# Batch 0's gated feed-forward in seven products instead of eight, and what moves on VectorE, GpSimd and the DMA queue for it

## The chip, the cores and the metric

One core of one Trainium2 chip runs the whole program. The metric is the device time in microseconds (us), median over several executions. Kernels of one call run on the same chip, with fresh runs of the kernel before among them.

## The reference, cut to what matters

```python
# q, k, v: (8 batches, 12 heads, 448, 64); w_gate, w_val: (768, 1536); w_out: (1536, 768)
scores = scale * q @ k.T - log(S);  attn = sigmoid(scores) @ v
x = attn as (8*448, 768)
y = (maximum(x @ w_gate, 0) * (x @ w_val)) @ w_out
```

The kernel takes four heads at a time: "block" n is four heads of one batch, three blocks to a batch, so batch 1 is blocks 3 to 5 and block 6 opens batch 2. The attention of batch b+1 ("visits") is spread among the feed-forward products of batch b.

The feed-forward has one trick. `x @ [w_gate, w_val]` and `h @ w_out` are done as 2 by 2 block products in the Strassen-Winograd way: seven block products instead of eight, with sums of the inputs, differences of the weights and sums of the results made on VectorE. "Product (g, k)" is product k of seven in group g of six.

## The kernel before: the parts that matter

Batch 0 uses plain products (eight), as the weights have only just arrived. Its stage is a time plan: each matmul has a cost, and loads, casts, visits and weight differences are dropped in between.

```python
def load_w(kind, j, half):                 # half a group of gate or value weights, staged as fp32
    st = swp.tile([P, WH], FP32, tag="sw") # five staging buffers of their own
    nc.sync.dma_start(st..., src...)
def cast_w(kind, j, half, eng): ...        # GpSimd casts it to fp16
def load_cast_out(f, eng):                 # one row of w_out: load, cast
    st = stp.tile([P, 2, S], FP32, tag="st")
    nc.sync.dma_start(flat, moe_w_out[f * P : (f + 1) * P, :])
    eng.tensor_copy(wo[:, f], flat)

def feed(i):                               # with each attention visit: what the next block needs
    ...
        if c == 4:
            dma_transposes(m)              # blocks 6 and later; blocks 4 and 5 go through TensorE
            if m == NPRO: order.extend(("o", f, 0) for f in range(NFC))   # then the rows of w_out
    if c == 4 and NPRO <= m + 1 < NB:
        load_all(m + 1)

for step, cost in enumerate(ffn0()):       # batch 0: plain products
    t += cost
    if order and (...): start_next()       # a load and its cast
    if due and t >= due[0]: visit()
    if wdue and t >= wdue[0]: gv_weights(*wsums.pop(0))
sums(("x", 1), [3, 2, 1, 4])               # input sums of batch 1, after all of batch 0
```

In a seven-product group the relu goes to one buffer, `r1`, and the first output product goes to GpSimd.

```python
elif k == 2: nc.scalar.activation(tmp(key, "r1")[:], ps, AF.Relu)          # bufs=1
elif k == 3: ...; nc.gpsimd.tensor_tensor(out=..., in0=r1, in1=s1, op=mult)
```

Of the kernel before, what the change touches and what calls it, by code (L numbers as in the profile page):

```python
# [16 lines left out]
def kernel(  # L17
# [10 lines left out]
    nc = tc.nc  # L28
# [21 lines left out]
    swp = ctx.enter_context(tc.tile_pool(name="swp", bufs=5))  # L50
# [14 lines left out]
    free = [0, 1]  # L65
# [20 lines left out]
    WH = NDC * FG * P // 2  # L86
# [3 lines left out]
    hT = wpool.tile([P, NFC, NHALF * S], FP16, name="hT")  # L90

# [6 lines left out]
    xT: dict = {}  # L98

# [44 lines left out]
    def load_w(kind: str, j: int, half: int):  # L144

        st = swp.tile([P, WH], FP32, tag="sw", name=f"st_w{kind}")
        w, r0 = moe_w_gate if kind == "g" else moe_w_val, half * NDC // 2 * P
        src = w[r0 : r0 + NDC // 2 * P, j * FG * P : (j + 1) * FG * P]
        nc.sync.dma_start(st[:].rearrange("p (c f) -> p c f", f=FG * P), src.rearrange("(c p) f -> p c f", p=P))
        staged[kind, j, half] = st  # L150

    def cast_w(kind: str, j: int, half: int, eng):
        st = staged.pop((kind, j, half))
        n = NDC // 2
        dst = (wg if kind == "g" else wv)[j][:, half * n : (half + 1) * n].rearrange("p c f -> p (c f)")
        eng.tensor_copy(dst, st[:])

    def load_cast_out(f: int, eng):

        st = stp.tile([P, 2, S], FP32, tag="st", name="st_wo")  # L160
        flat = st[:].rearrange("p r s -> p (r s)")[:, 0:DM]
        nc.sync.dma_start(flat, moe_w_out[f * P : (f + 1) * P, :])
        eng.tensor_copy(wo[:, f], flat)  # L163
# [11 lines left out]
    def transposes(n: int, nm: str, *engines, cut=(0, NCH)):  # L175
        h16 = qk16.pop((nm, n))
        if n <= NBLK:
            bank = take()
            tr = banks[bank][:, 0:S]
        else:  # L180
            bank = None
            tr = next_pair()[:, 0, 0:S]
        tr = tr.bitcast(FP16).rearrange("p (c h k) -> p c h k", c=NCH, h=2)
# [8 lines left out]
        if bank is not None:  # L192
            give(bank)
# [23 lines left out]
    def values(n: int, chunks):  # L217
        if chunks[0] == 0 and n not in PT:
            if n < NBLK:
                PT[n] = [banks[2][:, :], banks[3][:, :]]  # L220
# [17 lines left out]
        if chunks[-1] == NCH - 1:  # L238
# [12 lines left out]
            v16.pop(n)  # L251


    MM_US = 0.189

    begun: dict = {}

    def gv_part(b: int, f: int, w, dcs):

        key = (b, f, w is wg)  # L260
        if key not in begun:
            begun[key] = take()
        j, jj = divmod(f, FG)
        for dc in dcs:
            nc.tensor.matmul(  # L265
                banks[begun[key]][:, 0:S],
                w[j][:, dc, jj * P : (jj + 1) * P],
                xT[b, dc // 3][:, dc % 3],
                start=(dc == 0),
                stop=(dc == NDC - 1),  # L270
            )
        return begun[key]

    def up(b: int, f: int, gate_done=0, val_first=0):
        if val_first:
            gv_part(b, f, wv, range(val_first))
        for dc in range(gate_done, NDC):
            gate = gv_part(b, f, wg, [dc])
            if dc < NDC - 1:
                yield MM_US  # L280
        g_sb = tmpp.tile([P, S], FP32, tag="s2", name="gate_sb")
        if f < NFC // 2:
            nc.vector.tensor_scalar(out=g_sb[:], in0=banks[gate][:, 0:S], scalar1=0.0, scalar2=None, op0=AOP.max)
        else:
            nc.scalar.activation(g_sb[:], banks[gate][:, 0:S], AF.Relu)
        give(gate)
        yield MM_US
        for dc in range(val_first, NDC):
            val = gv_part(b, f, wv, [dc])
            if dc < NDC - 1:  # L290
                yield MM_US
        o = (b % NHALF) * S
        nc.vector.tensor_tensor(
            out=hT[:, f, o : o + S], in0=g_sb[:], in1=banks[val][:, 0:S], op=AOP.mult
        )
        give(val)
        yield MM_US
# [21 lines left out]
    def gv_weights(k: int, j: int):  # L319
# [8 lines left out]
        if i % 2 == 0:  # L328
            T["tile"] = swp.tile([P, 2, HDC, FG * P], FP16, tag="sw", name="Tw")
        T[k, j] = T["tile"][:, i % 2]  # L330
# [5 lines left out]
    def out_weights(k: int, part: int):  # L336
# [9 lines left out]
        elif k == 4:  # L346
            t = T["tile"][:, 1].rearrange("p c f -> p (c f)").rearrange("p (r m) -> p r m", m=HM)[:, 0:2]
# [119 lines left out]
    def out_product(pair: int, k: int):  # L467
# [29 lines left out]
        def store(t, m0, m1):  # L497
            for half in range(2):
                b, r = divmod((pair + t) * P + 64 * half, S)
                rows = out[b * S : (b + 1) * S].rearrange("(p c) m -> c p m", c=NCH)  # L500
                eng = nc.scalar if half and final and m0 == 0 and t == 1 else nc.sync
# [12 lines left out]
        elif k == 2:  # L514
            nc.scalar.activation(y(0)[:, 0:HM], ps, AF.Copy, scale=OUT_SCALE)
            give(i)
            if final:
                store(0, 0, HM)
        elif k == 3:
            scaled(y(0)[:, HM:DM], ps, live[key, "s1"][:, 0:HM])  # L520
            give(i)
            store(0, HM if final else 0, DM)
# [8 lines left out]
    def ffn(b: int, two_pairs):  # L531

        todo = [(0, 1), (0, 6), (0, 7), (0, 2), (0, 5), (1, 1), (0, 3)]
        for g in range(1, HFC):
            todo += [(g, 6), (g - 1, 4), (g, 7), (g, 5), (g, 2)]
            todo += [(g + 1, 1), (g, 3)]
        todo += [(HFC - 1, 4)]
        p, q_ = two_pairs
        for g, k in todo:
            if g == HFC:  # L540

                out_product(p, 1)
                yield OUT_US, False
                continue
            gv_product(b, g, k)
            if g == HFC - 1 and k == 5:
                sums(("h", p), [3])
            if g == HFC - 1 and k == 4:
                sums(("h", p), [2, 1, 4])
            yield GV_US, k in (2, 6)  # L550
        for i, k in (
            [(p, 7), (p, 2), (p, 6), (q_, 1), (p, 5), (q_, 6), (p, 3), (p, 4)]
            + [(q_, 7), (q_, 5), (q_, 2), (q_, 3), (q_, 4)]
        ):
            out_product(i, k)
            if (i, k) == (p, 6):
                sums(("h", q_), [3, 2])
            if (i, k) == (p, 5):
                sums(("h", q_), [1])
            if (i, k) == (p, 3):  # L560
                sums(("h", q_), [4])
            if b + 1 < B:
                if (i, k) == (q_, 5):
                    sums(("x", b + 1), [3, 2, 1])
                if (i, k) == (q_, 3):
                    sums(("x", b + 1), [4])
            yield OUT_US, True
# [3 lines left out]

    def cast_block(n: int):
        cast_qk(n, "q", nc.gpsimd)
        cast_qk(n, "k", nc.gpsimd)
        cast_v(n, nc.gpsimd)

    def feed(i: int):
# [3 lines left out]
        if NPRO <= m < NB:  # L581
# [6 lines left out]
            if c == 4:  # L588
                dma_transposes(m)
                if m == NPRO:  # L590
                    order.extend(("o", f, 0) for f in range(NFC))
        if c == 4 and NBLK < m < NPRO:
            later.append(m)
        if c == 4 and NPRO <= m + 1 < NB:
            load_all(m + 1)

    later: list = []
# [24 lines left out]

    zeros = hT[:, 0, 0:512]
    nc.vector.memset(zeros, 0.0)

    def filler(*widths):

        for w in widths:
            nc.tensor.matmul(banks[2][:, 0:w], zeros[:, 0:P], zeros[:, 0:w], start=True, stop=True)

    with tc.manual_schedule():
# [6 lines left out]

        def halves(kind, j):
            return [(kind, j, 0), (kind, j, 1)]  # L640

        order = halves("g", 0) + ["kq"] + halves("u", 0) + ["v", 4] + halves("g", 1) + halves("u", 1)
        order += [5] + halves("g", 2) + halves("u", 2)

        def start_next():
            what = order.pop(0)
            if isinstance(what, int):
# [142 lines left out]
```

## Time and profile before

| | before |
|---|---|
| time, median of 3 runs | 420.67 us |
| batch 1's first waiting product, (0, 6), starts | 73.33 us |
| product (2, 6) of batch 1 starts | 84.27 us |
| last batch starts its products | 375.5 us |

TensorE is the bound nearly everywhere and at full clock. Its two longest waits after the opening (timeline: start, length, what, and in brackets the idle time before it and what ended it) are

```profile
73.33 0.73 PE L402 MATMUL bank<-S,Tw 128*128 128x224 f16 x6 [2.73 <-DVE S L317]
84.27 0.73 PE L402 MATMUL bank<-S,Tw 128*128 128x224 f16 x6 [1.20 <-ACT r L445]
```

The first is for batch 1's input sums, the second for the relu buffer.

### The profile page before, as it was taken

What the parts mean: (1) busy time and instruction counts of PE and PEld (TensorE: products, weight loads), DVE (VectorE), ACT (ScalarE), POOL (GpSimd) and SP (SyncE); (2) the same over time, 40 slices, a digit from 0 to 9 for tenths busy, and PEclk for the clock granted to TensorE, in tenths of its full rate; (3) what the DMA queues carried; (4) which work ended last, traced back from release to release, by engine and by line L of the source; (5) the groups of instructions that cost most, each with busy time, mean ns of one, the idle gap of its engine ahead of it and who ended that gap; (6) DMA issues with size and microseconds to landing.
All of it is one profiled execution on the core that took longest, in us unless ns stands there. A gap on an engine that the chain in (4) does not pass through costs nothing.

```text
span 419.8 us, 9616 instructions
## 1 busy us (share of the span) xinstructions
PE 396.2 (94%) x3940; PEld 275.6 (66%) x3940; DVE 296.5 (71%) x471; ACT 237.7 (57%) x334; POOL 169.7 (40%) x185
## 2 busy tenths in 40 slices
PE   7869997897999999999999999999999999999994
PEld 3334443776558885588756887478865878569952
DVE  3555487879967778666875878566786767668882
ACT  5954775465645675467574656557664666533110
POOL 2667845863612534245341635305452352102310
PEclk9999999999999999999999999999999999999998
DMA  8999969375195634596064760867426860032006
GB/s 298 383 383 385 367 144 377 118 192 159 23 229 124 191 116 72 179 248 160 21 176 129 200 176 2 217 147 175 142 46 206 152 145 2 0 93 60 2 0 151
DMA packets 64636, 67.08 MB, mean 160 GB/s; under 512 B 35920, under 2 KB 55120, under 8 KB 64592
## 3 DMA queue, kind: packets, MB, share of 16 engines
q1 hardware_dynamic: 63424, 64.73, 54.4%
q10 hardware_dynamic: 1168, 1.74, 1.2%
q8 instruction: 31, 0.51, 0.5%
q14 instruction: 13, 0.11, 0.1%
HBM read 47.19 MB, written 11.01 MB: 139 GB/s over the span
## 4 chain that ended last, share of the span: by engine, by line
PE 72%; ACT 9%; DVE 7%; DMA 4%; issue 3%; POOL 2%; SPq 1%; ACTq 0%; DVEq 0%; POOLq 0%
PE bank L402 54%; PE pair L201 7%; ACT PT L211 6%; PE pair L229 6%; PE bank L265 4%; DVE s L317 3%; DMA st_wo<-in_moe_w_out_dram 3%; POOL wo L163 2%; ACT xT L247 1%; DMA st_q<-in_q_dram 1%; DVE hT L458 1%; DVE To L314 1%; ACT r L445 1%; ACT s L437 1%; PE bank L185 1%
## 5 line engine op out<-in xcount | busy, mean ns | idle before, releaser
L211 ACT ACTIVATE PT<-pair,bias_t 128x896 f16<-128x896 f32 x168 | 161.4, 1012 | 53.0 <-PE pair L201 53.0
L317 DVE TENSOR_TENSOR s<-bank,s 128x448 f32<-128x448 f32 x210 | 128.3, 621 | 49.8 <-PE bank L402 42.8
L451 POOL TENSOR_TENSOR hT<-r,s 128x448 f16<-128x448 f32 x42 | 47.7, 1137 | 166.7 <-DVE s L317 119.1
L402 PEld LDWEIGHTS <-Tw 128*128 128x128 f16 x756 | 71.2, 98 | 11.5 <-issue 11.4
L402 PE MATMUL bank<-S,Tw 128*128 128x224 f16 x504 | 62.0, 259 | 4.5 <-DVE S L317 2.7
L402 PE MATMUL bank<-S,wv 128*128 128x224 f16 x504 | 62.0, 259 | 2.5 <-DVE s L317 1.2
L402 PE MATMUL bank<-xT,wg 128*128 128x224 f16 x504 | 60.5, 259 | 0.9 <-DVE s L317 0.9
L201 PE MATMUL pair<-qT,kT 64*64 64x448 f16 x672 | 55.0, 364 | 5.9 <-ACT PT L211 5.2
L445 ACT ACTIVATE r<-bank 128x448 f32<-128x448 f32 x42 | 22.9, 544 | 58.4 <-PE bank L402 55.7
L402 PEld LDWEIGHTS <-wv 128*128 128x128 f16 x504 | 48.0, 98 | 7.3 <-issue 6.5
L402 PEld LDWEIGHTS <-wg 128*128 128x128 f16 x504 | 47.2, 98 | 7.3 <-issue 6.3
L402 PEld LDWEIGHTS <-S 128*128 128x128 f16 x336 | 30.7, 98 | 25.9 <-issue 4.7
L201 PEld LDWEIGHTS <-kT 64*64 64x64 f16 x672 | 18.3, 104 | 33.0 <-issue 27.8
L458 DVE SCALAR_TENSOR_TENSOR hT<-s,s 128x448 f16<-128x448 f32 x42 | 36.2, 863 | 1.4
L488 DVE SCALAR_TENSOR_TENSOR s<-bank,s 128x384 f32<-128x384 f32 x28 | 15.6, 556 | 29.5 <-PE bank L402 29.4
L402 PEld LDWEIGHTS <-hT 128*128 128x128 f16 x252 | 24.0, 98 | 16.4 <-issue 1.3
L132 POOL CAST h16q<-st_q 128x896 f16<-128x896 f32 x20 | 19.7, 987 | 35.4 <-issue 22.4
L247 ACT ACTIVATE xT<-pair 128x448 f16<-128x448 f32 x42 | 20.5, 541 | 21.1 <-PE pair L229 20.0
L402 PE MATMUL bank<-wo,hT 128*128 128x384 f16 x168 | 32.0, 327 | 0.1
L402 PE MATMUL bank<-wo,S 128*128 128x384 f16 x168 | 31.9, 326 | 0.0
L402 PE MATMUL bank<-To,S 128*128 128x384 f16 x168 | 31.3, 327 | 0.5 <-DVE S L317 0.5
L229 PE MATMUL pair<-PT,v 64*64 64x448 f16 x588 | 31.5, 350 | 0.0
(68 smaller groups left out, 423.0 us busy)
## 6 DMA issues: line engine op xcount, KB each, us to landing
st_q<-in_q_dram SPq DMA_DIRECT2D x23, 448.0 KB, 4.6
st_v<-in_v_dram SPq DMA_DIRECT2D x23, 448.0 KB, 5.4
out_dram<-ysb SPq DMA_DIRECT2D x52, 192.0 KB, 2.9
st_k<-in_k_dram SPq DMA_DIRECT2D x22, 448.0 KB, 4.1
st_wg<-in_moe_w_gate_dram SPq DMA_DIRECT2D x6, 768.0 KB, 11.9
st_wu<-in_moe_w_val_dram SPq DMA_DIRECT2D x6, 768.0 KB, 12.4
st_wo<-in_moe_w_out_dram SPq DMA_DIRECT2D x12, 384.0 KB, 6.1
out_dram<-ysb SPq DMA_DIRECT2D x7, 96.0 KB, 2.2
```

The costliest lines, as they stand in the source:

```text
L132: eng.tensor_copy(o, i)
L201: nc.tensor.matmul(ps[o : o + 64, bank, 0:S], kT[r : r + 64, c, h, :], qT[r : r + 64, :, h, :], start=True, stop=True, tile_position=(r, o ...
L211: nc.scalar.activation(pt[:], ps[:, :, 0:S], AF.Sigmoid, bias=bias_t[:], scale=qk_scale)
L229: nc.tensor.matmul(pv[pr][o : o + 64, 0:S], t[r : r + 64, pr, c * D : (c + 1) * D], pt[r : r + 64, pr, :], start=(c == 0), stop=(c == NCH ...
L247: nc.scalar.activation(x, pv[pr][:, 0:S], AF.Copy, scale=XSCALE)
L265: nc.tensor.matmul(banks[begun[key]][:, 0:S], w[j][:, dc, jj * P : (jj + 1) * P], xT[b, dc // 3][:, dc % 3], start=(dc == 0), stop=(dc == ...
L317: nc.vector.tensor_tensor(out=out, in0=a, in1=b, op=AOP.add)
L402: nc.tensor.matmul(bank[:, c0:c1], lhsT, rhs, start=(first and i == 0), stop=last, skip_group_check=True)
L445: nc.scalar.activation(tmp(key, "r1")[:], ps, AF.Relu)
L451: nc.gpsimd.tensor_tensor(out=out[:, :, o : o + HS], in0=two(live[key, "r1"]), in1=two(t), op=AOP.mult)
L458: nc.vector.scalar_tensor_tensor(out=out[:, :, o + HS : o + S], in0=two(t), scalar=0.0, in1=two(live[key, "s4"]), op0=AOP.max, op1=AOP.mult,)
L488: nc.vector.scalar_tensor_tensor(out=out, in0=ps, scalar=OUT_SCALE, in1=c, op0=AOP.mult, op1=AOP.add)
```

## The change

Its intent: batch 0 too in seven products (2.9 us less TensorE work), blocks 4 and 5 transposed by DMA and not on TensorE (2.4 us less), weights staged in places that later sums will use, all casts on GpSimd by a fixed plan, and four value banks taken in turn. The core of it, cuts marked:

```diff
-    swp = ctx.enter_context(tc.tile_pool(name="swp", bufs=5))
+    tw = [wpool.tile([P, 2, NDC // 2, FG * P], FP16, name=f"tw{i}") for i in range(5)]
+    homes = [wo[:, i * FG : (i + 1) * FG]... for i in range(3)] + [tw[i]... for i in (3, 4, 2)]
     ...
-            if i == 15: cast_qk(NBLK, "k", nc.vector)
-            if i == 17: cast_qk(NBLK, "q", nc.vector)
+            if i == 10:
+                cast_qk(NBLK, "k", nc.gpsimd); cast_qk(NBLK, "q", nc.gpsimd)
     ...
+        gv_product(0, 0, 7)
+        sums(("x", 0), [2, 1, 4])
+        sp_1 = [lambda: dma_transposes(m), lambda: load_w("u", 1, 0, 0), ...]
+        sp_2 = [lambda: dma_transposes(m + 1), lambda: load_w("u", 2, 0, 4), lambda: load_w("u", 2, 1, 0)]
+        sp_2 += [lambda: load_all(m + 1, "v"), lambda: load_all(NPRO)]
+        plan = {
+            0: [cq(m, "k"), cq(m, "q"), *sp_1],
+            1: [cw("g", 1, 0), gw(4, 0)],
+            ...
+            13: [cq(m + 1, "k"), gw(4, 1)],
+            14: [cq(m + 1, "q"), *sp_2],
+            ...
+            28: [cq(NPRO, "q"), lambda: dma_transposes(NPRO)],
+            29: [lambda: load_all(NPRO + 1)],
+            31: [lambda: cast_v(NPRO, nc.gpsimd)],
+        }
+        rows = list(range(NFC))
+        for i, x in enumerate(todo):        # seven-product groups of batch 0
+            one(x, behind)
+            ...
+            for do in plan.pop(i, []): do()
+            if i >= 29 and rows: load_cast_out(rows.pop(0))
     ...
-                eng = nc.scalar if half and final and m0 == 0 and t == 1 else nc.sync
+                eng = nc.scalar if half and final and m0 == 0 else nc.sync
```

## The prediction

> **What bounds the kernel now.** I read the page first, then busy times by stage, then the chain of waits where the stages differ, then the queue of the DMA issuer. The stages are cut where the first product of a batch stands on TensorE: attention of batch 0 up to about 30 us, FFN of batch 0 (plain products) from 30 to 69.9, FFN of batch 1 (seven products) from 69.9 to 127.4, then a steady period of 49.65 us per batch, and a last batch without attention.
>
> ```profile
> 30.00:69.90 39.90, 39.74 (x341) 18.78 (x340) 24.90 (x33) 27.14 (x35) 26.09 (x26) 1.00 0.93 316
> 69.90:127.40 57.50, 50.44 (x505) 35.61 (x504) 48.45 (x70) 30.23 (x43) 31.43 (x33) 1.00 0.55 154
> 127.40:177.10 49.70, 49.08 (x506) 35.77 (x505) 36.01 (x59) 30.21 (x43) 19.65 (x21) 1.00 0.54 144
> 35.00:50.00 15.00, 14.94 (x134) 7.05 (x132) 7.24 (x12) 10.02 (x13) 11.84 (x11) 1.00 1.05 384
> 50.00:57.00 7.00, 6.94 (x60) 3.32 (x57) 5.77 (x8) 5.57 (x7) 5.63 (x6) 1.00 0.40 133
> ```
>
> The columns are the stretch, its length, busy us of PE, PEld, DVE, ACT, POOL, then clock, DMA share, GB/s. Batch 0's FFN and the steady period are full of TensorE work. Batch 1's FFN is not: 57.5 us against 49.65 for the same products, so 7.85 us are lost there. And until 50 us the DMA engines are saturated at 384 GB/s. Why batch 1 loses time, the chain of waits says (start, us, what):
>
> ```profile
> 56.66 1.23 SPq L170
> 57.94 1.33 SPq L110
> 60.34 6.48 DMA st_wo<-in_moe_w_out_dram
> 67.29 5.64 POOL wo L163 x5
> 72.95 5.80 DMA st_wo<-in_moe_w_out_dram
> 78.80 0.83 POOL wo L163
> 80.45 0.83 POOL wo L163
> 81.28 1.27 POOL h16k L132
> 82.55 1.11 POOL hT L451
> 83.68 0.55 ACT r L445
> 84.27 0.73 PE bank L402 x6
> ```
>
> The output weights land late, GpSimd casts them row by row (twelve rows), the gate-times-value product of batch 1's first group stands behind the last cast in GpSimd's order, ScalarE's relu (one buffer r1) stands behind that product, and TensorE gets its bank only then, at 84.27, for product 6 of group 2. So around 60 to 84 us the end is set by DMA and GpSimd, not by TensorE.
>
> The price of a transpose by DMA, in the steady period, and the end of the kernel:
>
> ```profile
> 163.00:167.00 4.00, 3.60 (x27) 1.86 (x26) 2.49 (x5) 3.33 (x5) 1.28 (x2) 1.00 0.96 147
> 409.34 7.95 SPq L502 DMA_DIRECT2D out_dram<-ysb  x11
> ```
>
> A k/q pair is 2 x 128 x 896 x 2 bytes = 0.46 MB. In those 4 us 0.59 MB moved, of which 0.13 MB (0.3 us at 384 GB/s) were not the pair's. At a share of 0.96 the pair took 3.85 - 0.3 = 3.5 us of all the engines. The second line: the last stores leave the one queue at about 0.6 us each until 417.3, though the last sum (the chain's last piece) ended at 415.1.
>
> **What the Trainium skill says.** "Trainium Kernel Development and Optimization", Key Constraints: DMAs of all issuing engines run on the same 16 DMA engines and interleave. The trace agrees: share 1.05 with loads from two queues at the start. "DMA: Bandwidth & Descriptors", Latency and other measured facts, gives 261 GB/s for a DMA transpose; here it is 0.46 MB in 3.5 us, 131 GB/s, and I use the trace. "SBUF — State Buffer", SBUF: two separate sides: a VectorE operation with two SBUF inputs and a GpSimd operation lock each other out of a shared port. The trace agrees in size: a weight difference of 128x1536 takes 0.95 us while GpSimd is idle (61 to 66 us) and 1.31 to 1.79 us beside its casts. "Perfetto Trace Analysis", Tensor Engine Instruction: VectorE, ScalarE and GpSimd take instructions strictly in order; the chain above is that.
>
> **The change part by part.**
> TensorE. Removed: 144 matmuls of 448 columns at a step of 0.189 us (ten in 1.89 us), 27.2 us. Added: 42 products of 6 at 0.578 us, 24.3 us. So 2.9 us less. Four sets of seven transposes (blocks 4, 5) go, 0.6 us each with the switch, 2.4 us less. The wait of 2.73 us for the sums of batch 1 at 70.6 goes too: those sums now lie inside batch 0's last group. Floor of the two stages afterwards: 24.3 + attention 11.1 + 0.5 for batch 0, and 49.3 for batch 1, 85.2 us where it was 97.4.
>
> VectorE. Batch 0 had 18 operations at 0.62 us; it gets 30 sums at 0.6 (18.0) and 6 products at 0.9 (5.4). Four copies at 0.62 go. The built order puts between 30 us and the end of batch 0's FFN: these 23.4 us, 9 weight differences at about 1.4 beside a busy GpSimd (12.6), 7 input sums at 0.8 (5.6), one eviction 0.6: 42 us, against TensorE's 36. Batch 1 keeps 30 sums, 6 products, 8.4 us of output weight differences and about 13 us of sums and evictions: 45 us. Together 87 us, so VectorE is nearly as long as TensorE's floor and in one order with it.
>
> GpSimd. Batch 0 brings 6 products at 1.14, 6.8 us, and the casts of block 3 from VectorE, 1.9 us.
>
> DMA. The loads up to all gate and value weights are the same 17.7 MB, which landed at 50.5 us. After them, or among them, must still come: block 6 (1.38 MB), block 7, which the built order loads twice (24 loads each of q, k, v on that queue where there were 23: both the plan and the visit issue it), 2.75 MB, and 4.72 MB of output weights; 4.13 MB at 384 and 4.72 at 406 GB/s (65 to 72 us) are 22.4 us. And three transposed pairs instead of one stand ahead of them in the queue: 10.5 us. The queue doesn't idle long (it waits for casts of keys while eight loads are outstanding), so the last row of output weights can't land before 50.5 + 22.4 + 10.5 = 83.4 us. Before it landed at 78.7.
>
> The chain. The built order on GpSimd has the rows interleaved with what TensorE waits for: rows 0 and 1, v of block 6, row 2, product of group 4 of batch 0, rows 3 to 5, a cast of q, rows 6 to 9, product of group 5, rows 10 and 11, a cast of k, product of group 0 of batch 1. Row 1 lands ten rows (9.7 us) before the last, at 73.7. Then, at 0.96 us a cast (median): row 1 74.6, v 76.5, row 2 77.5, product 78.6; three rows, q, four rows, product: 87.4; two rows 89.3, k 90.5, product 91.7, relu 92.3. So product 6 of group 2 in batch 1 starts between 83.4 + 0.83 + 1.3 + 1.14 + 0.55 = 87.2 (casts all keeping up) and 92.3, where it started at 84.27: 3 to 8 us later. What follows it is the same work, 43.1 us before, of which 2.5 us were short waits for VectorE; I take 0.5 off. So +2.5 to +7.5 at the start of batch 2.
>
> Steady batches: TensorE's own work is 49.3 of 49.65 us, so the new order of visits is worth at most 0.3 each either way; I put 0. The end: the last pair has four stores on the SP queue instead of seven, three at 0.6 off, of which about 1.5 count before the last sum sets the end. Prologue: the value banks in turn take away 0.71 and 0.15 us waits, but all of it lies before the DMA-bound point, so 0. Sum: +1 to +6, middle +3.5.
>
> **The rivals.**
> A, TensorE's floor: weights are in time and the new sums hide. Then two stages take 85.2 plus some 2 us of waits instead of 97.4, with the end 12 us less: 409. For it: TensorE is the longest chain by far (72%). Against: the DMA share of 1.05 and the chain through GpSimd above.
> B, VectorE becomes the bound: 87 us of work plus idle as in batch 1 before (57.5 - 48.45 = 9 us, part of which is filled now, say 7), 94 instead of 97.4, and 1.5 at the end: 416. For it: VectorE was already 84% busy in batch 1's stage and its operations take longer beside GpSimd.
> C, DMA and GpSimd as worked out: 424. For it: the bytes don't change, the pairs and the second load of block 7 only add. Against: casts could keep up better, or the queue's order could overlap pairs with loads more than in the steady period; a planned change is also seldom made to lose.
>
> **Range and chances.** I give C about 65%, B 25%, A 10%. Weighed, the middle is 423 us, 0.5% slower. Faster by 2% means under 412.3: A and the best of B, 0.12. Slower by 2% means over 429.1: the far end of C, 0.08. Within: 0.80. Eight in ten: 412.5 to 429.
>
> **What would show it.** Right: DMA share near 1 almost without a gap up to 80 us; the last output row landing at 83 or later; GpSimd idle some 5 to 10 us before row 1; a TensorE wait of 1 us or more behind ScalarE's r in batch 1's first two groups; product 6 of group 2 at 87 to 92 us; the start of batch 2 at 130 to 135; the last store issued within 1 us after the last sum. Wrong: rows landing before 80 us (the pair's price is off), GpSimd without idle, or VectorE as the releaser all through 30 to 80 us (then B), or batch 2 starting before 120 us (then A).

## More of the kernel before

Calls ran on different chips: the kernel before had medians of 420.39 to 421.9 us in them, so differences of medians between calls carry about 1 us of doubt, and the ratios decide.

From the page of the kernel before: busy time by engine, the granted clock of TensorE in 40 slices, and the shares of the chain that ended last.

```profile
PE 396.2 (94%) x3940; PEld 275.6 (66%) x3940; DVE 296.5 (71%) x471; ACT 237.7 (57%) x334; POOL 169.7 (40%) x185
PEclk9999999999999999999999999999999999999998
PE 72%; ACT 9%; DVE 7%; DMA 4%; issue 3%; POOL 2%; SPq 1%; ACTq 0%; DVEq 0%; POOLq 0%
```

## The result, and the profile after

The changed kernel took 440.08 us (439.49 to 440.86, 4 runs), the kernel before 420.89 us beside it: a ratio of 1.0445, 95% interval 1.0404 to 1.0485, slower. The prediction's main case had the direction right, and the chain that it named (late rows, GpSimd, relu, TensorE) stands in the trace, though at another product than it worked out; its 423 us and the top of its range, 429, were far too low.

Where the time went is quickly found: the last batch starts at 394.26 instead of 375.5 us (+18.8), the period of the steady batches is nearly the same (49.7 against 49.6 us), and the end is 0.7 us shorter (43.64 instead of 44.3 us). Nearly all of it, 18.0 us, was lost before batch 1's product (0, 6), at 91.32 instead of 73.33 us. The same three lines of the page after:

```profile
PE 395.4 (90%) x4020; PEld 284.8 (65%) x4020; DVE 304.9 (70%) x487; ACT 239.4 (55%) x340; POOL 181.7 (42%) x193
PEclk9968998959999999999999999999999999999999
PE 68%; DVE 9%; DMA 8%; POOL 6%; issue 3%; ACT 2%; SPq 2%; DVEq 0%; POOLq 0%; ACTq 0%
```

TensorE's busy time fell by only 0.8 us, not by the 5.3 that the change takes off, and its clock shows dips to 5, 6 and 8 tenths in the first quarter. TensorE's longer waits in the changed kernel:

```profile
26.37 0.93 PE L184 MATMUL bank<-ident,h16k 128*128 128x128 f16 x7 [2.90 <-POOL h16k L136]
37.42 1.40 PE L356 MATMUL bank<-S,tw 128*128 128x224 f16 x12 [3.11 <-DVE s L273]
...
63.23 0.73 PE L356 MATMUL bank<-S,wv 128*128 128x224 f16 x6 [2.43 <-DVE s L273]
65.55 1.09 PE L356 MATMUL bank<-S,tw 128*128 128x224 f16 x6 [1.58 <-DVE tw L270]
91.32 1.28 PE L356 MATMUL bank<-S,tw 128*128 128x224 f16 x6 [10.42 <-ACT r L399]
99.41 0.73 PE L356 MATMUL bank<-S,tw 128*128 128x224 f16 x6 [1.45 <-ACT r L399]
```

The 10.42 us is a wait for the predicted releaser, ScalarE's relu, in one of the two groups that the prediction named. It stands at (0, 6) behind the output product of batch 0's group 4, though, and not at (2, 6) behind batch 1's group 0; (2, 6) itself started without a wait, at 104.65 us. And there are other waits ahead of it. See also the durations: six matmuls take 1.28 us at 91.32, where the kernel before took 0.73. The windows (length, busy us of PE, PEld, DVE, ACT, POOL, then clock, DMA share, GB/s) show why:

```profile
24.00:26.00 2.00, 0.00 (x0) 0.00 (x0) 1.52 (x1) 0.64 (x1) 2.00 (x2) 0.71 1.05 378
28.00:30.00 2.00, 2.00 (x18) 1.24 (x15) 2.00 (x3) 0.94 (x1) 1.89 (x3) 0.50 1.04 383
92.00:94.00 2.00, 2.00 (x16) 0.81 (x14) 0.71 (x2) 0.83 (x1) 2.00 (x4) 0.50 0.81 264
```

After the longer waits the clock is halved, and stays so for several us although TensorE is full again. The Trainium skill states this in "TensorE: Matmul & The Clock Gate", Part 1 ("What's actually happening"): an idle array goes back to half rate. The trace agrees, 0.50 in the second and third line. An estimate of what it cost: in each 2 us window from 24 to 98 us with a clock below 1, busy time times (1 - clock); 24 to 32 give 2.6 us, 38 to 42 give 1.7, 66 to 70 give 1.6, 90 to 98 give 2.6, together 8.5 us. So the wait of 2.90 us at 26.37 was paid nearly twice, that of 3.11 us and the pair of 2.43 and 1.58 us about one and a half times, and that of 10.42 us one and a quarter times; after the wait of 1.73 us at 48.38 the clock stayed at 1.00. (Against the 5.3 us that the change takes off, busy time came out only 4.5 us too long. The estimate and this figure were not reconciled.)

Why the 10.42 us: the queue of the DMA issuer (SPq; the transposes of blocks 5 and 6 are the DMA_TRANSPOSE pairs, of which only the first of a pair is shown; "..." marks cuts).

```profile
37.00 0.55 SPq L153 DMA_DIRECT2D tw<-in_moe_w_gate_dram  x1
52.76 1.23 SPq L174 DMA_TRANSPOSE kT<-h16k  x1
...
55.37 0.58 SPq L153 DMA_DIRECT2D tw<-in_moe_w_val_dram  x1
...
58.45 0.48 SPq L114 DMA_DIRECT2D st_v<-in_v_dram  x1
69.98 1.23 SPq L174 DMA_TRANSPOSE kT<-h16k  x1
...
72.60 0.57 SPq L114 DMA_DIRECT2D st_k<-in_k_dram  x1
...
74.26 0.47 SPq L166 DMA_DIRECT2D st_wo<-in_moe_w_out_dram  x1
74.77 0.52 SPq L114 DMA_DIRECT2D st_k<-in_k_dram  x1
...
76.38 16.98 SPq L166 DMA_DIRECT2D st_wo<-in_moe_w_out_dram  x11
```

From 37.6 to 52.8 and from 58.9 to 70.0 us the queue issues nothing: at its head stands a transpose that waits, in the end for a cast on GpSimd. The view of waits, for the issuer of the DMA queue, adds that 7.8 us of the first stretch went by before TensorE had finished reading the tile that the transpose writes into, and 7.3 us on the cast; in the second stretch the tile cost 1.0 us. What was queued before went on landing meanwhile. The DMA share of the two stretches is the last figure but one of each line below; without new loads the engines stood still from about 48 to 54 us (share 0.03 or less) and from about 66.5 to 70 us:

```profile
37.50:52.80 15.30, 13.27 (x140) 9.50 (x140) 10.68 (x15) 9.34 (x12) 9.38 (x9) 0.89 0.68 248
58.90:70.00 11.10, 7.09 (x74) 4.01 (x72) 7.09 (x8) 4.23 (x7) 8.47 (x9) 0.85 0.71 262
```

The third value weights (55.37) and the rows of the output weights (74.26 on) stand behind such a transpose. Keys of block 7 go out twice, at 72.60 and 74.77. In the kernel before, the rows stood behind block 6's pair as well, but that pair went out at 55.23 us and the rows from 60.34 on:

```profile
55.23 1.32 SPq L170 DMA_TRANSPOSE kT<-h16k  x1
60.34 13.98 SPq L162 DMA_DIRECT2D st_wo<-in_moe_w_out_dram  x12
```

And on GpSimd, in the changed kernel:

```profile
68.29 1.66 POOL L136 CAST h16k<-st_k 128x896 f16<-128x896 f32 x1
...
81.57 0.83 POOL L167 CAST wo<-st_wo 128x768 f16<-128x768 f32 x1 [10.74 <-DMA st_wo<-in_moe_w_out_dram]
86.17 0.83 POOL L167 CAST wo<-st_wo 128x768 f16<-128x768 f32 x1 [3.78 <-DMA st_wo<-in_moe_w_out_dram]
...
89.58 1.12 POOL L405 TENSOR_TENSOR hT<-r,s 128x448 f16<-128x448 f32 x1
```

The cast of block 6's keys, 68.29 to 69.95, releases the queue at 69.98. (The view of waits names the queries' cast, but that ended 0.85 us after the issue. In the kernel before, the keys' cast ended at 55.20; the changed kernel's plan places it at step 26 of batch 0.) The cast of the queries follows, and then GpSimd has nothing to do for 10.74 us until the first row lands, and the output product of group 4 waits behind rows 0 to 2 until 89.58, which releases the relu and then TensorE at 91.32.

### The profile page after: what moved, and what is told of

It is laid out like the page before. It is cut to its first block, busy times and chain, and to the rows that moved or that the text cites. A ratio compares the mean times of both kernels' runs of the same rounds, so it can differ in the third digit from the quotient of the medians.

```text
span 437.9 us, 9783 instructions
## 1 busy us (share of the span) xinstructions
PE 395.4 (90%) x4020; PEld 284.8 (65%) x4020; DVE 304.9 (70%) x487; ACT 239.4 (55%) x340; POOL 181.7 (42%) x193
## 4 chain that ended last, share of the span: by engine, by line
PE 68%; DVE 9%; DMA 8%; POOL 6%; issue 3%; ACT 2%; SPq 2%; DVEq 0%; POOLq 0%; ACTq 0%
PE bank L356 55%; PE pair L199 7%; PE pair L228 6%; DVE s L273 3%; DMA wo<-in_moe_w_val_dram 3%; DVE S L273 2%; DVE hT L412 2%; DMA st_v<-in_v_dram 2%; POOL wo L167 2%; DMA st_wo<-in_moe_w_out_dram 2%; DMA st_k<-in_k_dram 2%; ACT PT L209 1%; SPq L174 1%; POOL hT L405 1%; POOL h16k L136 1%
## 5 line engine op out<-in xcount | busy, mean ns | idle before, releaser
L273 DVE TENSOR_TENSOR s<-bank,s 128x448 f32<-128x448 f32 x240 | 145.9, 622 | 80.6 <-PE bank L356 73.4
L405 POOL TENSOR_TENSOR hT<-r,s 128x448 f16<-128x448 f32 x48 | 55.4, 1153 | 200.7 <-DVE s L273 173.3
L356 PEld LDWEIGHTS <-tw 128*128 128x128 f16 x864 | 81.6, 99 | 29.7 <-issue 24.9
L356 PE MATMUL bank<-S,tw 128*128 128x224 f16 x576 | 72.4, 263 | 18.5 <-ACT r L399 11.9
L356 PE MATMUL bank<-S,wv 128*128 128x224 f16 x576 | 72.2, 262 | 4.3 <-DVE s L273 4.2
L356 PE MATMUL bank<-xT,wg 128*128 128x224 f16 x576 | 68.1, 262 | 0.0
L356 PEld LDWEIGHTS <-wv 128*128 128x128 f16 x576 | 55.3, 99 | 10.0 <-issue 8.2
L356 PEld LDWEIGHTS <-wg 128*128 128x128 f16 x576 | 54.5, 99 | 7.3 <-issue 6.2
L356 PE MATMUL bank<-xT,tw 128*128 128x224 f16 x288 | 36.2, 262 | 0.0
L391 ACT COPY s<-bank 128x448 f32<-128x448 f32 x48 | 25.9, 539 | 15.2 <-DVE S L270 11.9
```

The source lines that it names most:

```text
L273: nc.vector.tensor_tensor(out=out, in0=a, in1=b, op=AOP.add)
L356: nc.tensor.matmul(bank[:, c0:c1], lhsT, rhs, start=(first and i == 0), stop=last, skip_group_check=True)
L391: nc.scalar.copy(tmp(key, "s1")[:], ps)
L405: nc.gpsimd.tensor_tensor(out=out[:, :, o : o + HS], in0=two(live[key, "r1"]), in1=two(t), op=AOP.mult)
```

## The experiments

Three theories for the 18.7 us, to be told apart. H: the head of the queue, and with it late rows. L: bytes and transposed pairs on the DMA engines (what the prediction worked out). V: the pace of VectorE and GpSimd in batch 0's new stage. All runs of the changed kernel's variants:

| run | median us | ratio to before (95%) |
|---|---|---|
| changed kernel | 440.08 | 1.0445 (1.0404 to 1.0485) |
| load_once | 437.17 | 1.0353 (1.0300 to 1.0406) |
| pe_transposes | 440.69 | 1.0449 (1.0394 to 1.0504) |
| loads_first | 438.65 | 1.0389 (1.0329 to 1.0448) |
| products_first | 438.83 | 1.0403 (1.0354 to 1.0452) |
| rows_early | 433.43 | 1.0285 (1.0235 to 1.0335) |
| rows_early_load_once | 430.72 | 1.0215 (1.0161 to 1.0269) |
| sums_later | 427.89 | 1.0149 (1.0104 to 1.0194) |
| keys_first | 430.15 | 1.0221 (1.0156 to 1.0286) |
| keys_on_dve | 430.31 | 1.0234 (1.0183 to 1.0285) |
| thirds_first | 430.33 | 1.0203 (1.0166 to 1.0241) |
| casts_on_act | 432.73 | 1.0288 (1.0254 to 1.0321) |
| doubled | 436.29 | 1.0384 (1.0329 to 1.0438) |
| fewer (result wrong) | 427.71 | 1.0174 (1.0144 to 1.0204) |
| fewer_thirds_first (wrong) | 428.34 | 1.0176 (1.0147 to 1.0204) |
| fewer_pe_transposes (wrong) | 426.41 | 1.0089 (1.0047 to 1.0130) |

### One edit each to the changed kernel

**load_once**: block 7 is loaded by its visit alone.

```diff
-            29: [lambda: load_all(NPRO + 1)],
```

> The changed kernel with block 7 loaded once (1.38 MB less between rows 0 and 1 of the output weights). Theory H (the load queue is held at its head by transposes that wait for casts, so the rows of output weights are issued only from 74 us on, and from there they come as fast as the DMA engines move bytes): row 1 lands some 3.6 us earlier, and since GpSimd's product of group 4 stands behind row 2, the kernel gains about 3.5 us: 436.5 us. Rival B (the DMA engines' total of bytes is too large from the start): the same 3.6 us. Rival V (VectorE's added sums and the lowered clock are the loss, 30 to 70 us): 0, 440 us.

437.17 us, as expected. The wait for the relu buffer shrank from 10.42 to 6.06 us. A useless 1.38 MB in front of most of the rows costs some 3 us (the intervals of the two ratios just touch).

**pe_transposes**: blocks 4 and 5 on TensorE again.

```diff
-        sp_1 = [lambda: dma_transposes(m), lambda: load_w(...
+        sp_1 = [lambda: load_w(...          # sp_2 likewise; transposes(n, "k"), transposes(n, "q") at steps 8 and 21
```

> The changed kernel with blocks 4 and 5 transposed by TensorE again, as before the change; one of its parts undone alone. H: the loads of the second and third value weights, of v and of blocks 5 and 6 no longer stand behind a wait for casts in the queue (15 us with nothing issued from 37.5 to 52.8 us), so the third weights come some 10 us earlier, the waits of TensorE at 63 and 65 us (2.4 and 1.6) go, and the transposes of block 6 are issued at about 64 instead of 70 us: 5 to 7 us gained less 2.4 us of TensorE: 435 to 437 us. B: two pairs of 3.5 us less for the DMA engines: 7 us less 2.4, also about 435, but then the DMA share is near 1 all the way and the rows move by 7 us. V: 2.4 us more on TensorE and four copies on VectorE: 442 to 443 us.

440.69 us, no gain: a miss. Two pairs fewer, but the transposes of block 6 still went out at 69.6 us, as the cast of block 6's keys that they wait for (68.62 to 69.54 us) has its place in GpSimd's order. So the rows came no earlier than 73.9 us, and TensorE waited 7.62 us and did more transposes besides.

**loads_first**: the transposes of blocks 4 and 5 stand behind their step's loads in the queue (block 4's still ahead of the third gate weights).

```diff
-        sp_2 = [lambda: dma_transposes(m + 1), lambda: load_w("u", 2, 0, 4), ... lambda: load_all(NPRO)]
+        sp_2 = [lambda: load_w("u", 2, 0, 4), ... lambda: load_all(NPRO), lambda: dma_transposes(m + 1)]   # sp_1: behind load_all(m + 1, "kq")
```

> The changed kernel with the same transposes by DMA, but each pair behind the loads of its step in the queue (same bytes, same instructions on all engines, another order on one queue). H: as much gained as with TensorE's transposes and none of their cost: 4 to 7 us, 433 to 436 us. B: nothing, 440 us, because no byte is saved. V: nothing, 440 us. A miss of H in the other direction: 442 or more if the transposes now come too late for the scores of block 5.

438.65 us, a miss for the same reason: the transposes of block 6 went out at 69.78, 0.02 us after the cast of its keys. It is that pair, not those of blocks 4 and 5, that the rows wait behind.

**products_first**: on GpSimd the row casts come after all of batch 0's gate-times-value products, and the output weights' differences come later in batch 1.

```diff
-            if i >= 29 and rows: load_cast_out(rows.pop(0))     # all rows after the loop
-                    if late: late.pop(0)()
+                if late and (...) and t > (5 if len(late) == 7 else 11): late.pop(0)()
```

> The changed kernel with the casts of the output weight rows behind all of batch 0's products in GpSimd's order, and the weight differences of the output later in batch 1, as before the change. Theory P (the place of the row casts ahead of the gate products in GpSimd's order is what turns late rows into a wait of TensorE): the wait of 10.4 us behind ScalarE's r at 80.9 us goes, and one of 3 to 6 us comes where the first product of batch 1 stands behind row 11: 4 to 7 us gained, 433 to 436 us. If the rows' lateness were only covered by another bound (V), 438 us or more.

438.83 us, a miss in size. The wait of 10.42 us is gone (1.77 us, for VectorE, is left at 85.06), but one of 5.70 us for the same relu buffer came at 98.45: the rows are needed by then, and they are as late as ever. Order on GpSimd alone only moves the wait.

### The rows, the second load and the input sums

**rows_early**: loads of the first five rows ahead of block 6's transposes in the queue; their casts stay where they were.

```diff
+            25: [gw(2, 2), *(lambda f=f: load_out(f) for f in range(5))],   # load_cast_out split in two
```

> The changed kernel with the loads of rows 0 to 4 of the output weights put in the queue before the transposes of block 6 (nothing else; their casts stay where they were). Theory H2, formed after the first four runs (the rows are late because their loads are issued behind block 6's transposes, which wait until 69.9 us for the cast of block 6's q, and that cast is late by GpSimd's and VectorE's own pace, not by the queue, which is why putting loads before the transposes of blocks 4 and 5 gave nothing): rows 0 to 2 are there before GpSimd asks for them at 70.8, the product of group 4 ends near 76 instead of 90.7, the wait of 10.4 us at 80.9 goes nearly whole; 428 to 431 us. Rival L (the load of the late rows only moves: rows 5 to 11, behind block 7 twice, then hold the product of group 5 as long): 436 us or more.

433.43 us, 6.7 less, between the two expectations. The output product of group 4 runs at 76.63 instead of 89.58 us and no wait for the relu is left before batch 1's group 2, where 2.62 us come back at 92.61 for the rows that still go behind the pair. So the head of the queue is what made this wait (H), and 6.7 us of the loss are its.

**rows_early_load_once**: both edits.

> The same with block 7 loaded once. H2: what is left of waiting for rows 5 to 11 goes: 0 to 2 us less than with the early rows alone (the 3.5 us of the single load are mostly already in the early rows): 427 to 430 us. L: the full 3.5 us again, 433.

430.72 us: they add up (2.7 us more, every run below every run of rows_early, though the intervals of the ratios overlap), and the wait for the relu is down to 0.85 us. So most of the remaining 9 us must lie elsewhere.

**sums_later**: rows_early_load_once, and batch 0's last input sum with one weight difference moved behind the first result sums. In the changed kernel the 3.11 us at 37.42 had come from these: of three sums the first began as a cast of GpSimd did and took 0.51 us, and two that began inside a cast took over three times that (from VectorE, then GpSimd).

```profile
32.08 0.51 DVE L273 TENSOR_TENSOR S<-xT,S 128x672 f16<-128x672 f16 x1
32.51 1.77 DVE L273 TENSOR_TENSOR S<-xT 128x672 f16<-128x672 f16 x1
34.20 1.76 DVE L270 TENSOR_TENSOR S<-xT,S 128x672 f16<-128x672 f16 x1
32.09 3.52 POOL L160 CAST wg<-tw 128x1536 f16<-128x1536 f32 x2
```

```diff
-        sums(("x", 0), [2, 1, 4])
+        sums(("x", 0), [2, 1])              # [4] at step 2, gw(4, 0) at step 3
```

> The same, and on VectorE the last input sum S4 and the weight difference 4 of the first third stand behind the first sum that frees a bank (before: three sums at up to 1.8 us and a difference ahead of it, and TensorE idle for 3.1 us at 34.3). Theory V2 (with the rows in time, batch 0's FFN is set by VectorE beside GpSimd, so a wait taken from its start shows at the end): 2 to 3 us less, 425 to 427 us. Rival W (the work only moves: VectorE is full anyway until 80 us): under 1 us.

427.89 us, 2.8 less, the size expected (again every run below every run of rows_early_load_once, with overlapping intervals). The first wait, 2.73 us in rows_early_load_once, is 1.01 us at 34.61 and 0.72 us at 37.82, and the clock from 30 to 40 us rose from 0.88 to 0.98. Batch 1's (0, 6) now starts at 80.57 us: still 7.2 later than before the change. That rest, 6.5 us of time, is the subject of most other runs.

**keys_first** and **keys_on_dve**: block 3's keys and queries cast earlier on GpSimd, or on VectorE as the kernel before has it (both on sums_later).

> The same, and k and q of block 3 are loaded and cast ahead of the first value weights, so that TensorE's transposes don't wait for them (2.9 us idle at 23.4, after which the trace shows a granted clock of 0.74 from 20 to 30 us). Theory C (the idle time takes the clock down and costs on): 3 us and the slow matmuls of 26 to 33 us, 3 to 5 us less: 421 to 424 us, and a clock of 1.00 from 20 to 30. Rival: the first value weights come 2.4 us later and VectorE's first differences with them: 0 to 1 us less.

> As sums_later (427.89 us), but keys and queries of block 3 are cast on VectorE and loaded ahead of the first value weights, as the kernel before has them. Their wait on GpSimd was 1.96 us in sums_later, after which the clock stood at 0.85 for ten us. If that wait and its clock are a loss of their own: the wait goes, the clock of 20 to 30 us is above 0.95, 425 to 426.5 us. Rival: VectorE is late there already, so the wait comes back behind it, 427.3 us or more.

430.15 and 430.31 us, both misses. With keys_first the wait for GpSimd at 26 us went, but one of 1.94 us for VectorE came at 18.85 in the attention, which ran some 2.4 us later. With keys_on_dve 3.31 us behind VectorE stood in the old wait's place. Why the kernel before can do these casts on VectorE without such a wait was not settled; it has no weight differences there.

### What sets the pace of batch 0's stage

**thirds_first**: sums_later with the transposes of blocks 4 and 5 behind the loads in the queue. **casts_on_act**: that, and six weight casts on ScalarE.

```diff
-            nc.gpsimd.tensor_copy(dst, st)
+            nc.scalar.copy(dst, st)         # second value, third gate and value weights
```

> The changed kernel with everything that the run sums_later has (early rows, one load of block 7, input sums in turn), and the transposes of blocks 4 and 5 issued behind their step's loads, so that the third value weights need not wait for a cast of queries. In sums_later TensorE still waited 2.66 us and 1.89 us near 60 to 63 us, for VectorE differences that stood behind the casts of the third value weights, which waited for their DMA until 57.6 and 60.2 us; the clock was 0.66 in the ten us after. Theory Q (queue: a late load, then the clock): both waits go, the clock stays at 1.00 there, batch 1's product (0,6) starts near 76 to 78 instead of 80.57, and the time is 423 to 425 us (427.9 before it). Rival V (VectorE's own pace with nine differences and thirty sums): the waits come back within 5 us behind VectorE, the start stays at 79.5 or later, 427 us or more.

> As thirds_first (430.33 us), but the six casts of second value, third gate and third value weights run on ScalarE, which is 44 to 78 per cent busy there, and not on GpSimd. In thirds_first the third value weights had landed early, but their casts still ran at 58.3 and 60.1 us, behind a product that waited 3.48 us for VectorE in GpSimd's order. Theory G (GpSimd's order and its beats with VectorE set batch 0's stage): the TensorE waits of 1.73 and 1.58 us near 63 to 66 us go, the differences of VectorE come down towards 0.95 us each, batch 1's product (0,6) starts at 78.5 or earlier instead of 82.64, 424 to 427 us. Rival V (VectorE's own sums, with TensorE back and forth over four banks): VectorE stays the releaser, 428.5 us or more; casts on ScalarE may also hold up its copies and sigmoids, then a ScalarE releaser shows and the time goes up.

430.33 and 432.73 us, both misses. In thirds_first the third value weights were in place early, but their casts ran at 58.32 and 60.13 us, as late as in sums_later (57.64 and 60.20), because GpSimd waited 3.48 us for VectorE's sum ahead of them; and TensorE waited 1.38 us for block 5's pair. On ScalarE the casts stood behind the sigmoids, and TensorE's wait for a weight difference grew to 4.53 us. Theory G, that GpSimd need only be relieved, fell.

**doubled**: sums_later with six weight differences done twice.

```diff
         subtract(T[k, j], a, b)
+        if j: subtract(T[k, j], a, b)
```

> As sums_later (427.89 us), with six of the nine weight differences in batch 0's stage done twice (the result stays right): some 7 us more of VectorE work at 1.2 us each. If VectorE's work bounds the stage (rival B of the prediction): 432.5 to 435 us. If it does not and the waits for it are only waits for late weights: 430 us or less.

436.29 us, 8.4 more; VectorE's busy time rose by 9.0 us on the page (304.7 to 313.7), more than the 7 us expected. Added VectorE work costs about its whole length here. **fewer** asks the reverse: four of the nine differences left out, with a wrong result.

```diff
+        if j and k in (1, 4): T[k, j] = T.get((2, j)); return    # the second difference's tile in their place
```

> As sums_later (427.89 us), with four of the nine weight differences in batch 0's stage left out (second and third weights: the first and fourth difference are replaced by the second's tile), so the RESULT IS WRONG ON PURPOSE; TensorE, DMA and GpSimd do the same work. Some 4.8 us less of VectorE at 1.2 us each. The doubled run showed that VectorE's added work costs its full length; this asks whether taking it away gives it back. If VectorE's work bounds the stage: 422.5 to 425 us, and TensorE's waits for differences near 45.6 and 63.4 us shrink. If something else stands right behind it (late third value weights, GpSimd's order): 426 us or more.

427.71 us: nothing won, with 5.2 us less of VectorE's busy time. TensorE's wait at 63.48 even grew to 6.09 us, and behind VectorE stood GpSimd, and behind it the DMA (PE, then POOL of this run):

```profile
63.48 1.30 PE L368 MATMUL bank<-S,tw 128*128 128x224 f16 x6 [6.09 <-DVE tw L276]
```

```profile
57.53 1.47 POOL L160 CAST wv<-tw 128x1536 f16<-128x1536 f32 x1 [2.06 <-DMA tw<-in_moe_w_val_dram]
60.64 1.47 POOL L160 CAST wv<-wo 128x1536 f16<-128x1536 f32 x1 [1.64 <-DMA wo<-in_moe_w_val_dram]
```

So a second limit seems to stand beside VectorE: the third value weights, whose loads wait in the queue behind block 5's transposes. **fewer_thirds_first** takes both away, **fewer_pe_transposes** takes the pairs of blocks 4 and 5 off the queue instead (both wrong).

> Both edits together: four weight differences left out (WRONG RESULT on purpose, as fewer) and the third value weights' loads ahead of the transposes in the queue (as thirds_first). Each alone won nothing over sums_later (427.7 and 430.3 against 427.9). If two limits of about equal length stand beside one another in batch 0's stage (VectorE's differences and the arrival of the third value weights), then both together win: TensorE's wait of 6.09 us at 63.5 falls under 2.5 us, batch 1's product (0,6) starts at 77.5 or earlier, 422.5 to 425.5 us. If GpSimd's order is a third limit (the casts run at 58 to 60 us although the weights have landed), the wait stays above 3 us and the time at 427 or more.

> As fewer (four weight differences left out, WRONG RESULT on purpose; 427.71 us), with blocks 4 and 5 transposed on TensorE again, as pe_transposes did it: four sets of seven transposes more on TensorE (2.4 us), four copies of 0.62 us more on VectorE, and no transposed pair between a cast of queries and the loads of value weights. In fewer the third value weights were cast at 57.5 and 60.6 us as they landed and TensorE waited 6.09 us at 63.5; with the loads put ahead of the pair TensorE waited 4.59 us for the pair. If the pair and the loads compete in the one queue and are the limit that stands beside VectorE: third value weights cast by 58, no wait above 2.5 us between 50 and 70 us, batch 1's product (0,6) at 78 or earlier and 423 to 426 us. If not: a wait of 3 us or more remains there, 427 or more.

With the loads first, 428.34 us: another miss. The weights were cast by 58.6 us, but now the pair was late. With the pairs on TensorE, 426.41 us, a ratio of 1.0089 where fewer had 1.0174. The two runs' longest waits of that stretch:

```profile
60.43 0.40 PE L205 MATMUL pair<-qT,kT 64*64 64x448 f16 x4 [4.59 <-DMA qT<-h16q]
```

```profile
61.77 0.75 PE L374 MATMUL bank<-S,tw 128*128 128x224 f16 x6 [1.97 <-DVE tw L282]
```

In fewer_pe_transposes the clock stayed at 1.00 from 50 to 80 us and batch 1's (0, 6) started at 75.61 us, 5 us earlier than in sums_later, in spite of 2.4 us more TensorE work. This fits two limits side by side in this stage, VectorE's differences and the contest of a transposed pair with value weights on one queue. It does not show them: the run that would, sums_later with the pairs on TensorE and all nine differences kept, was not made, so taking the pairs off the queue may have won this alone (pe_transposes had it only with the rows still late). Against fewer the gain is clear of the intervals, against sums_later (1.0104 to 1.0194) it is not. The time is 0.4 us above the expected range because the later rows, behind block 6's pair, then stop GpSimd for 3.60 us, and TensorE waits 2.62 us for the relu at 84.68.

### The kernel before, with what was learnt

**rows_early on the kernel before**: five rows loaded at 44 us, where its queue idles until 55.23 (10.6 us of it, by the view of waits, for the tile that the transpose writes into, then for the cast).

```diff
             load_all(m + 1)
+            if m + 1 == NPRO:
+                for f in range(5): load_out(f)
```

> The kernel BEFORE the change, with one edit: the loads of the first five rows of the output weights are issued right behind the loads of block 6 (near 44 us, where its queue idles until 55 us for a cast), and not behind the transposes of block 6 and the loads of block 7. Their casts stay where they were. If the head of the queue is what sets the rows' time in this kernel too: GpSimd's nine us without work before its first row cast go, the last row is cast near 76 to 78 us instead of 81.3, product 6 of group 2 in batch 1 starts at 79 to 81 instead of 84.27, and the time is 416.5 to 418.5 us (421.3). Rival: batch 1 is short of VectorE as well, so the waits of 0.3 to 0.8 us grow and less than 1.5 us is won, 419.5 or more.

419.70 us, ratio 0.9963 (0.9934 to 0.9992): the expectation missed, its rival's figure held. TensorE's waits in this run from 30 to 95 us: the 1.20 us for the relu at 84.27 is gone, the other two kinds are as before.

```profile
72.98 0.73 PE L408 MATMUL bank<-S,Tw 128*128 128x224 f16 x6 [2.39 <-DVE S L323]
75.71 0.73 PE L408 MATMUL bank<-S,Tw 128*128 128x224 f16 x6 [0.24 <-DVE s L323]
94.17 0.73 PE L408 MATMUL bank<-S,wv 128*128 128x224 f16 x6 [0.78 <-DVE s L323]
```

The gain of 1.7 us is about that of TensorE's wait and its neighbour's shrinking (2.73 to 2.39), not that of GpSimd's nine idle us: the rest of the chain's lateness had been slack.

**rows_sums** moves batch 1's input sums into batch 0's last products, **rows_sums_stores** adds the changed kernel's final stores.

```diff
-        due = [3.0 + k * (total - 3.0 - 2.5) / (n - 1) for k in range(n)]
+        due = [3.0 + k * (total - 3.0 - 4.5) / (n - 1) for k in range(n)]
                 visit()
+                if not due: sums(("x", 1), [3, 2, 1, 4])
-        sums(("x", 1), [3, 2, 1, 4])        # at the end
```

> As rows_early on the kernel before, and the input sums of batch 1 are put right behind batch 1's last attention visit, with the visits ending 2 us earlier in batch 0, so that they lie inside the last plain products. This is the one term of the change that took away a TensorE wait (2.73 us at 70.6). If that wait is worth its length: 1.5 to 2.7 us less than rows_early, 414 to 416.5 us. If the rows' chain sets the end of that stretch anyway, the wait only moves behind it: within 0.7 us of rows_early.

> As rows_sums, with the changed kernel's final stores (first tile of the last pair stored whole after its last sum, its second half issued by ScalarE). Measures the tail term alone: the prediction had 1.5 us, the changed kernel's trace shows 0.66 us from the start of the last batch to the end. Expected 0.4 to 1.5 us less than rows_sums, 413 to 416 us; if the four stores collide at the end, no gain.

417.09 us (0.9909, 0.9878 to 0.9941) and 416.55 us (0.9886, 0.9863 to 0.9909). Product (0, 6) now starts without a wait at 69.30 us, and the edit won 2.6 us, about the length of the old wait; it moved the visits too, and 1.03 us behind VectorE is left at product (0, 5). Both times are some 0.6 us above the ranges expected. The stores' 0.5 us has overlapping intervals and is not settled. The last one beats both kernels, by 1.1% of the kernel before.

## Why the prediction was wrong, by its own steps

- **TensorE, "2.9 us less" and "2.4 us less".** The counts stand, but busy time fell by only 0.8 us over the kernel. The prediction took matmul durations at full clock; after the longer waits it was 0.50, an estimated 8.5 us. No term of the sum had this, nor the waits of TensorE from 26 to 66 us (2.90, 3.11, 1.73, 0.86, 2.43 and 1.58 us).
- **DMA, "the queue doesn't idle long ... so the last row ... can't land before 83.4".** This is the step that failed in the main case. It took the engines as busy throughout and counted bytes; the queue stood still for 15.2 and 11.1 us behind transposes that waited for a tile and for casts, and the DMA share was 0.68 and 0.71 in those stretches. The first row was issued at 74.26 us and the last at 93.0, when by the sum all should have landed for 9.6 us. Row 1 was cast at 86.17 where the prediction had it land at 73.7. Rows_early (6.7 us) confirms it; pe_transposes, which takes away two of the "3.5 us" pairs and has the first row issued at 73.93, shows that the time the pairs took on the engines was not what delayed the rows.
- **Block 7 loaded twice.** Seen, and right: counted as 1.38 MB in the sum, it measured 2.9 us.
- **The chain.** Right in its links: rows, output product, relu, TensorE. Wrong in its place: with row 1 landing 12.5 us early in the sum, the product of group 4 was worked out for 78.6 us, with no wait counted for it; it ended at 90.7 and held TensorE at (0, 6). Product (2, 6) started at 104.65 us, not 87.2 to 92.3, and batch 2 at 145.7, not 130 to 135.
- **VectorE, "nearly as long as TensorE's floor".** The two were worked out as 42 and 36 us for batch 0's stage, and then only the DMA's end was carried forward, as if these two would hide one behind the other. They did not: TensorE waited for VectorE's difference, VectorE for GpSimd's cast (1.71 us at 61.68), GpSimd for VectorE's sum (0.81 us at 56.94, 3.48 in thirds_first), each in order. The rest of 6.5 us in sums_later is this stage; doubled shows that VectorE's work counts there, fewer that it is not the only limit.
- **Input sums "at 0.8".** Two took 1.77 and 1.76 us beside GpSimd; moving one, with a weight difference, won 2.8 us.
- **"Prologue: 0".** Wrong: with block 3's casts on GpSimd TensorE waited 2.90 us for them, and the clock was halved until about 31 us (the kernel before waited 1.54 us near there, at full clock). Two attempts to win it back failed.
- **Rivals.** A and B both put the time below the kernel before. B was right that VectorE's work counts (doubled), wrong that the stage costs its busy time: fewer took 5.2 us of it away and won nothing. No rival let two causes add, though both had evidence in the profile. The direction was not luck, as the rows and the second load are terms of the sum (6.7 and 2.7 us of loss); but the other half, 2.8 and 6.5 us, came from what the sum did not hold.
- **The end, -1.5.** 0.7 us in the trace; about half.
- **Steady batches, 0.** Right: 49.7 against 49.6 us each.
- The prediction also said of the kernel before that from 60 to 84 us "the end is set by DMA and GpSimd, not by TensorE". The chain of waits follows the last arrival, but TensorE's own wait at its end was 1.20 us, and rows_early on the kernel before won 1.7.

Of the 18.7 us, then: rows behind the head of the queue 6.7, the second load 2.7, the placing of the input sums 2.8, and 6.5 in batch 0's stage, where none of the edits made to sums_later with a right result won anything. How the last divides among VectorE, the pairs and block 3's casts stays open.

## What to carry to other kernels

On an in-order queue, ask of each entry what it waits for, its source and the tile that it writes into, before counting the bytes behind it: put loads that need nothing ahead of a transfer that waits. When work is taken off the busiest engine and given to two others that feed each other in order, add up the waits of the loop and not the busy times, and look in the windows after each longer wait of TensorE for a halved clock: here it came after 2.90 and 3.11 us, and after two shorter waits close together, but not after 2.73. Check a chain of waits against the idle time of the engine at its end before believing that it is worth shortening.

## What the Trainium skill lacked or had wrong

- "TensorE: Matmul & The Clock Gate", Part 1 and "Why this matters for your kernels", warn of idle gaps above some 3 us. The length of one gap did not settle it here: a wait of 2.73 us left the clock at 1.00 (kernel before, at 73 us), one of 2.90 us brought it to 0.50 (changed kernel, 26 to 30 us), and so did waits of 2.66 and 1.89 us with 0.88 us of matmuls between (sums_later, 62 to 68 us). Whether the idle share of a longer stretch decides was not tested.
- "DMA: Bandwidth & Descriptors", Latency and other measured facts: 261 GB/s for a DMA transpose, measured on another kernel; the pair of 0.46 MB took an estimated 3.5 us here, 131 GB/s, as the prediction worked out.
- No page has a size for what a transpose that waits, for its source or for the tile that it writes into, does to the loads behind it in the issuer's order: 15.2 and 11.1 us without an issue in the changed kernel, 11 us in the kernel before.
- "SBUF — State Buffer", SBUF: two separate sides, gives the rule of the shared port but no size for a sum like those here: one of 128x672 fp16 took 0.51 us when it began as a GpSimd cast did and 1.77 us when it began inside one.
